# Banked sums, an early schedule and a third batch transposed by DMA in a windowed-attention and feed-forward kernel

## Chip, cores and metric

One core of a Trainium2 chip. The metric is the device time in microseconds (us) of one execution. "Faster" or "slower" needs 2%. Each kernel was profiled once; an instruction is named by its line in that run's kernel, so the same instruction has another line number in another run.

## The reference, cut

```python
# q, k, v: (8 batches, 8 heads, 576 positions, 64); each position sees those within 32
scores = where(|i-j| <= 32, q @ k.T / 8, -1e9);  attn = softmax(scores) @ v
x = attn.transpose(0, 2, 1, 3).reshape(4608, 512)
h = x @ w_in                                     # 512 -> 2048
g = where(h >= 1, h, where(h <= -1, 0, (h + 1) ** 2 / 4))
out = g @ w_out                                  # 2048 -> 512, float32
```

## The kernel before

Attention is woven into the feed-forward part. One pass of the main loop (here: a **slot**, 144 of them and 12 more for the tail) multiplies one 256-wide piece of w_in with 256 tokens (8 matmuls into `hp`), forms g on ScalarE and VectorE, and from slot 12 on adds 4 matmuls of the second product (`op`). Tables say in which slots the pieces of attention come: transposes of q and k, scores, masks, and sums (numerator and denominator of the softmax), whose result goes into `xT`, the left side of the first product.

```python
LONG, NAT = 2, 3            # batches 0, 1: transposed on TensorE from a long layout;
                            # batch 2: on TensorE; batches 3 and up: by DMA
...
def xpose(b, t):            # whole batch, DMA transpose on Sync's queue
    nc.sync.dma_start_transpose(out=qkT(b, t)..., in_=(qn, kn)[t][b]...)
...
def sums(b, y1, lo, hi, pool=ps_n):
    bb = two_banks(pool)    # pool has one buffer: two PSUM banks
    ...                     # matmuls with ones and with v into bb
    def end():
        A.activation(lr, bb[...], AF.Ln); A.activation(rc, lr, AF.Exp, scale=-1.0)
        muls.append(lambda: V.tensor_mul(o, bb[...], rc))   # into xT; done at the next slot's flush()
    return end
...
at(4, None, (0, (0, 1), (0, 2), (2, 4)))                       # slot, sums, scores
at(5, (0, 0, TB, MAIN), (0, (1, 2), (0, 2), (2, 4)))
at(6, (0, 1, TB, MAIN), (0,))
at(7, (0, 0, MAIN, S), None)
sl = [12, 13, 21, 23, 25, 27, 29, 32, 35, 39, ...]             # slots of the later sums
...
for n in range(3):
    tps[22 + n] = [(2, n, t) for t in range(2)]                # batch 2 on TensorE
for b in range(2, B):
    a = 12 if b == 2 else sl[5 * (b - 1) - 1] - 17             # 22 for batch 3, 39 for batch 4
    for t in range(3):
        loads.setdefault(a + t, []).append((b, t))             # q, k, v, issued by GpSimd
    for t in range(2):
        if b >= NAT:
            xps.setdefault(a + 9 + 2 * t, []).append((b, t))   # 31 and 33 for batch 3
...
A.activation(rr, hp, AF.Relu, scale=0.5, bias=0.5)             # every slot
V.tensor_max(hp, hp, rr)                                       # PSUM
V.scalar_tensor_tensor(gT[...], rr, 1.0, hp, op0=ALU.min, op1=ALU.mult)
```

The softmax here doesn't subtract the row's maximum and nothing guards it: scores larger than these inputs give would overflow.

## Time and profile before

| | before |
|---|---|
| median of 4 runs | 331.63 us (329.86 to 333.2) |
| span of the profiled run | 328.8 us |
| TensorE busy | 302.5 us, 92% |
| starts of slots 4, 8, 14, 27, 40 | 26.96, 38.91, 52.42, 84.58, 111.27 us |

The start of a slot is that of its first hp matmul in the trace; all 1152 of them are recorded. Two rows of the table of groups, their columns line, engine, operation, out<-in, shapes and count, then busy us and the mean ns of one, then idle time before them:

```profile
L419 DVE TENSOR_TENSOR hp<-hp,rr 128x512 f32<-128x512 f32 x144 | 100.5, 698 | 45.6 <-ACT rr L418 43.6
L420 DVE SCALAR_TENSOR_TENSOR gT<-rr,hp 128x512 bf16<-128x512 f32 x144 | 98.9, 687 | 4.9
```

They are the two VectorE instructions of each slot, 698 and 687 ns as means, together less than a slot's 1.74 us of matmuls.

### The profile page before, as it was taken

How to read it: one execution, taken by the hardware profiler on the slowest of the kernel's cores; microseconds unless marked ns; L12 is line 12 of the kernel's file. 1: busy time of each engine (PE TensorE's matmuls, PEld its weight loads, DVE VectorE, ACT ScalarE, POOL GpSimd, SP SyncE). 2: the span in 40 equal slices, each digit the busy share in tenths (PEclk: the TensorE clock that was granted, in tenths of full speed). 3: DMA queues.
4: the chain of work that ended last, by engine and by line, in shares of the span. 5: the costliest groups of instructions: out<-in, count | busy, mean ns of one | idle time of the engine just before them, and what ended most of it. 6: DMA issues, size and time to landing. Idle time of an engine off the chain costs nothing.

```text
span 328.8 us, 8409 instructions
## 1 busy us (share of the span) xinstructions
PE 302.5 (92%) x3572; PEld 202.4 (62%) x3615; DVE 227.7 (69%) x346; ACT 195.4 (59%) x320; POOL 140.8 (43%) x138
## 2 busy tenths in 40 slices
PE   7876599997999999999999999998999999999995
PEld 3354466665666666666666666666666666666652
DVE  2345577666678777777777778777677877787830
ACT  3647495675776566755766656665576666644421
POOL 8775717376535482549331962168231322100000
PEclk9989899999999999999999999999999999999999
DMA  7999999969918997699952999339950000010011
GB/s 126 147 171 147 146 205 111 165 64 168 103 52 159 105 131 130 129 106 111 165 84 62 108 157 153 73 50 169 170 106 33 35 34 35 34 63 32 34 64 64
DMA packets 128485, 34.52 MB, mean 105 GB/s; under 512 B 117696, under 2 KB 123584, under 8 KB 128448
## 3 DMA queue, kind: packets, MB, share of 16 engines
q0 software_dynamic: 99584, 18.06, 74.8%
q1 hardware_dynamic: 28864, 15.93, 19.5%
q8 instruction: 28, 0.46, 0.6%
q14 instruction: 9, 0.07, 0.1%
HBM read 36.70 MB, written 9.44 MB: 140 GB/s over the span
## 4 chain that ended last, share of the span: by engine, by line
PE 71%; ACT 8%; POOL 7%; issue 7%; DVE 3%; DMA 3%; ACTq 0%; POOLq 0%
PE hp L414 31%; PE op L432 31%; PE bb L276 5%; DMA w_in<-in_moe_w_in_dram 3%; ACT pt L224 2%; PE bb L216 2%; POOL vn L103 2%; ACT rr L418 1%; PE tp L181 1%; ACT lr L282 1%; DVE hp L419 1%; POOL pt L226 1%; ACT osb L436 1%; DVE gT L420 1%; DVE xT L288 1%
## 5 line engine op out<-in xcount | busy, mean ns | idle before, releaser
L414 PE MATMUL hp<-xT,w_in 128*128 128x256 bf16 x1152 | 151.4, 275 | 8.8 <-DMA w_in<-in_moe_w_in_dram 2.0
L414 PEld LDWEIGHTS <-w_in 128*128 128x128 bf16 x1152 | 111.7, 99 | 52.8 <-issue 9.2
L432 PE MATMUL op<-w_out,gT 128*128 128x512 bf16 x535 | 137.7, 379 | 5.7 <-issue 5.4
L418 ACT ACTIVATE rr<-hp 128x512 f32<-128x512 f32 x144 | 85.6, 595 | 94.2 <-PE hp L414 91.5
L419 DVE TENSOR_TENSOR hp<-hp,rr 128x512 f32<-128x512 f32 x144 | 100.5, 698 | 45.6 <-ACT rr L418 43.6
L420 DVE SCALAR_TENSOR_TENSOR gT<-rr,hp 128x512 bf16<-128x512 f32 x144 | 98.9, 687 | 4.9
L226 POOL TENSOR_TENSOR pt<-pt,mask 128x1024 bf16<-128x1024 bf16 x25 | 53.4, 2138 | 94.3 <-ACT pt L224 89.4
L432 PEld LDWEIGHTS <-gT 128*128 128x128 bf16 x576 | 53.3, 98 | 42.1
L288 DVE TENSOR_TENSOR xT<-bb,rc 128x512 bf16<-128x512 f32 (+1 forms) x32 | 21.0, 657 | 25.0 <-ACT rc L283 25.0
L224 ACT ACTIVATE pt<-bb 128x1024 bf16<-128x1024 f32 (+1 forms) x33 | 33.1, 1010 | 6.2 <-PE bb L216 4.3
L436 ACT COPY osb<-op 128x512 f32<-128x512 f32 x36 | 20.9, 582 | 14.8 <-PE op L432 14.5
L103 POOL DMA_DIRECT2D vn<-in_v_dram x32 | 27.5, 898 | 0.0
L283 ACT ACTIVATE rc<-lr 128x512 f32<-128x512 f32 (+2 forms) x40 | 23.5, 587 | 1.3
L276 PE MATMUL bb<-pt,ones 64*64 64x256 bf16 (+3 forms) x352 | 19.7, 256 | 4.4 <-DVE xT L288 3.6
L282 ACT ACTIVATE lr<-bb 128x512 f32<-128x512 f32 (+2 forms) x40 | 22.0, 550 | 2.1 <-PE bb L276 2.0
L276 PE MATMUL bb<-pt,vn 64*64 64x128 bf16 (+3 forms) x712 | 18.5, 204 | 0.5 <-DMA vn<-in_v_dram 0.5
L276 PEld LDWEIGHTS <-ones 64*64 64x64 bf16 x352 | 10.6, 105 | 13.1 <-issue 10.5
L244 POOL TENSOR_TENSOR pt<-pt,mask 128x384 bf16<-128x384 bf16 x7 | 6.4, 912 | 26.2 <-ACT pt L242 26.2
L276 PEld LDWEIGHTS <-vn 64*64 64x64 bf16 x712 | 16.8, 107 | 0.7 <-DMA vn<-in_v_dram 0.7
L87 POOL DMA_DIRECT2D kn<-in_k_dram x16 | 8.7, 549 | 17.2 <-DMA w_out<-in_moe_w_out_dram 9.1
L95 POOL DMA_DIRECT2D qn<-in_q_dram x12 | 15.0, 1254 | 1.0 <-issue 1.0
L95 POOL DMA_DIRECT2D kn<-in_k_dram x12 | 14.8, 1245 | 0.0
(46 smaller groups left out, 104.5 us busy)
## 6 DMA issues: line engine op xcount, KB each, us to landing
out_dram<-osb SPq DMA_DIRECT2D x36, 256.0 KB, 2.3
vn<-in_v_dram POOLq DMA_DIRECT2D x32, 144.0 KB, 8.1
qn<-in_q_dram POOLq DMA_DIRECT2D x12, 288.0 KB, 6.2
kn<-in_k_dram POOLq DMA_DIRECT2D x12, 288.0 KB, 8.4
w_in<-in_moe_w_in_dram POOLq DMA_DIRECT2D x8, 256.0 KB, 7.7
w_out<-in_moe_w_out_dram POOLq DMA_DIRECT2D x4, 512.0 KB, 11.2
kn<-in_k_dram POOLq DMA_DIRECT2D x16, 72.0 KB, 4.7
qn<-in_q_dram POOLq DMA_DIRECT2D x12, 72.0 KB, 7.7
```

The source lines that it names most:

```text
L95: nc.gpsimd.dma_start(out=x[:, :, h], in_=src[b, NY * h:NY * h + NY].rearrange("y s d -> (y s) d") .rearrange("(u p) d -> p u d", p=128))
L103: nc.gpsimd.dma_start(out=x[64 * a:64 * a + 64, :, h], in_=v[b, y:y + 2].rearrange("y s d -> (y s) d") .rearrange("(c r) d -> r c d", r=64))
L224: A.activation(p, ps[:, :, :128 * n].rearrange(like, y=m), AF.Exp, scale=D ** -0.5)
L226: eng.tensor_mul(p, p, mask4[:, :256 * n].rearrange("p (h j) -> p h j", h=2).rearrange(like, y=m))
L276: nc.tensor.matmul(bb[HD[h], a, o + c0:o + c1], ones[HD[a]] if c is None else vn[b][HD[a], c, h], p(a, h), start=n == 0, stop=True, skip_g ...
L282: A.activation(lr[:, :, :D0], bb[:, :, D0:2 * D0], AF.Ln)
L288: muls.append(lambda: V.tensor_mul(o, bb[:, :, :D0], rc[:, :, :D0]))
L414: nc.tensor.matmul(hp[:, j], w_in[:, kk, 256 * f + 128 * j:256 * f + 128 * j + 128], xT[:, kk, r0:r0 + TB], start=n == 0, stop=n == 3)
L418: A.activation(rr, hp, AF.Relu, scale=0.5, bias=0.5)
L419: V.tensor_max(hp, hp, rr)
L420: V.scalar_tensor_tensor(gT[t][:, 2 * f:2 * f + 2], rr, 1.0, hp, op0=ALU.min, op1=ALU.mult)
L432: nc.tensor.matmul(op, gT[tt // 2][:, ff, 128 * (tt % 2):128 * (tt % 2) + 128], w_out[:, ff], start=ff == 0, stop=ff == 2 * NF - 1)
```

## The change

It is meant to take TensorE's early waits away: sums get a second pair of banks where two follow each other, each transposed part gets its own bank, the early sums move a slot forward, v and the first piece of w_in come sooner, batch 2's transposes leave TensorE, and hp's banks come free one VectorE instruction earlier. The diff, cut:

```diff
-    LONG, NAT = 2, 3
+    LONG = 2
@@ early loads
+    load_v(0, (0,))                      # first half of v ahead of the identity
     make_identity(nc, ident)
-    load_v(0)
-    load_w_in(0)
+    load_v(0, (1,))
+    load_w_in(0, 0, 256)
+    load_w_in(0, 256, 512)
+    load_w_in(1)
     load_long(0, 1, 0)
-    load_w_in(1)
     load_long(0, 1, 1)
@@ schedule
-    at(4, None, (0, (0, 1), (0, 2), (2, 4)))
-    at(5, (0, 0, TB, MAIN), (0, (1, 2), (0, 2), (2, 4)))
-    at(6, (0, 1, TB, MAIN), (0,))
-    at(7, (0, 0, MAIN, S), None)
+    at(4, (scores, 0, (0, 1), (0, 2), (2, 4)), (scores8, 0, ps_n))
+    at(5, (sums, 0, 0, TB, MAIN), (scores, 0, (1, 2), (0, 2), (2, 4)))
+    at(6, (sums, 0, 1, TB, MAIN, ps_s), (sums, 0, 0, MAIN, S))
...
+    at(12, seq[0][0])
+    at(13, (*seq[1][0], ps_s))
+    for n, a in enumerate((20, 22, 25, 29)):       # sums of batch 1's rest, batch 2's first
+        at(a, seq[2 + n][0])
+    for n, a in enumerate((10, 11, 19, 20, 21, 27, 28)):   # scores; batch 2's first at 27, 28
+        at(a, seq[n][1])
...
-    for n in range(3):
-        tps[22 + n] = [(2, n, t) for t in range(2)]
...
-        a = 12 if b == 2 else sl[5 * (b - 1) - 1] - 17
+        a = (12, 26)[b - 2] if b < 4 else sl[5 * (b - 1) - 7] - 17
...
-            if b >= NAT:
-                xps.setdefault(a + 9 + 2 * t, []).append((b, t))
+            xps.setdefault(23 + t if b == 2 else a + 9 + 2 * t, []).append((b, t))
@@ slot
-        eng = None if a < 20 else P
+        eng = None if a < 21 else P
-            V.tensor_max(hp, hp, rr)
-            V.scalar_tensor_tensor(gT[t][:, 2 * f:2 * f + 2], rr, 1.0, hp, op0=ALU.min, op1=ALU.mult)
+            mx = ewp.tile([128, 2, TB], FP, name="mx")
+            V.tensor_max(mx, hp, rr)
+            V.scalar_tensor_tensor(gT[t][:, 2 * f:2 * f + 2], rr, 1.0, mx, op0=ALU.min, op1=ALU.mult)
```

More of the change, by code (lines that the diff above doesn't have):

```diff
@@ L96, in load_nat, with load_v @@
                                 .rearrange("(u p) d -> p u d", p=128))
-    def load_v(b):
-        x = vn[b] = nat.tile([128, 2 * NC, 2, D], BF, name="vn", tag="vn", bufs=3)
-        for h in range(2):
+    def load_v(b, hs=(0, 1)):
+        if b not in vn:
+            vn[b] = nat.tile([128, 2 * NC, 2, D], BF, name="vn", tag="vn", bufs=3)
+        x = vn[b]
+        for h in hs:
             for a in range(2):
@@ L104, in load_v, with load_w_in @@
                                     .rearrange("(c r) d -> r c d", r=64))
-    def load_w_in(n):
-        f = slice(512 * n, 512 * n + 512)
+    def load_w_in(n, c0=0, c1=512):
+        f = slice(512 * n + c0, 512 * n + c1)
         for h in range(2):
@@ L160 @@
     HD = (slice(0, 64), slice(64, 128))
+    HD = (slice(0, 64), slice(64, 128))
     def tpose(b, n, t, copy, ps):
-        o = qkT(b, t)
-        if b < LONG:
-            half, part = divmod(n, 2)
-            j0, j1 = ((0, 5), (5, 9))[part]
-            src = (qn, kn)[t][b, half]
-            dst = o.rearrange("d (y l p j) -> d l y p j", l=2, p=32, j=9)[:, half, :, :, j0:j1]
-            i = ps[:, :j1 - j0].rearrange("d j (y p) -> d y p j", y=NY)
-        else:
-            j0, j1 = 6 * n, 6 * n + 6
-            src = (qn, kn)[t][b].rearrange("p j h d -> p j (h d)")
-            dst = o[:, 128 * j0:128 * j1]
-            i = ps[:, :6].rearrange("d j p -> d (j p)")
+        half, part = divmod(n, 2)
+        j0, j1 = ((0, 5), (5, 9))[part]
+        src = (qn, kn)[t][b, half]
+        dst = qkT(b, t).rearrange("d (y l p j) -> d l y p j", l=2, p=32, j=9)[:, half, :, :, j0:j1]
         for j in range(j0, j1):
-            if len(src.shape) == 3 and b < LONG and src.shape[1] == 2:
+            if src.shape[1] == 2:
                 for h in range(2):
@@ L183, in tpose @@
                 nc.tensor.transpose(ps[:, j - j0], src[:, j], ident)
-        return lambda: copy(dst, i)
+        return lambda: copy(dst, ps[:, :j1 - j0].rearrange("d j (y p) -> d y p j", y=NY))
     def xpose(b, t):
@@ L226, in scores, with scores8 @@
             eng.tensor_mul(p, p, mask4[:, :256 * n].rearrange("p (h j) -> p h j", h=2).rearrange(like, y=m))
-    def scores8(b, eng):
+    def scores8(b, eng, pool=ps_s):
         p = pt8[b] = ptp.tile([128, 2, 2, TAIL], BF, name="pt8")
-        ps = two_banks(ps_s)
+        ps = two_banks(pool)
         if eng is None:
@@ L299, with tp1 @@
     TB = 256
-    def tp1():
-        return ps_h.tile([128, 8, 128], BF, name="tp", tag="hp")
-    def tp2(pool):
-        return pool.tile([128, 2, 8, 128], BF, name="tp", tag="bb")
+    def tp1(pool):
+        if pool is ps_h:
+            return pool.tile([128, 8, 128], BF, name="tp", tag="hp")
+        return pool.tile([128, 2, 8, 128], BF, name="tp", tag="bb")[:, 0]
     def keep_warm(n, pool, tag):
@@ L328 @@
         qn[0, 0] = cast(q32, "qb", 5)
-        qq = [tpose(0, n, 0, (A.copy, V.tensor_copy)[n], tp1()) for n in range(2)]
+        qq = [tpose(0, n, 0, (A.copy, V.tensor_copy)[n], tp1(ps_h)) for n in range(2)]
         for x in qq:
             x()
-        kk = tp2(ps_p)
-        c0, c1 = (tpose(0, n, 1, (A.copy, V.tensor_copy)[n], kk[:, n]) for n in range(2))
+        kk = [tpose(0, n, 1, (A.copy, V.tensor_copy)[n], tp1((ps_n, ps_p)[n])) for n in range(2)]
         keep_warm(3, ps_h, "hp")
-        c0()
-        c1()
+        for x in kk:
+            x()
         for m, n, w in ((mask4, 8, 128), (mask8, 4, TAIL)):
@@ L358, with at @@
     ev, tps = {}, {}
-    def at(a, su, sc):
-        assert a not in ev
-        ev[a] = su, sc
+    def at(a, *todo):
+        ev.setdefault(a, []).extend(x for x in todo if x)
     def steps(b, cut):
@@ L367, in steps @@
             for y1 in range(2):
-                yield (b, y1, lo, hi), (b, (y1, y1 + 1), (0, 2), (2 * k, 2 * k + 2))
-        yield (b, 0, MAIN, S), (b,)
-    at(4, None, (0, (0, 1), (0, 2), (2, 4)))
-    at(5, (0, 0, TB, MAIN), (0, (1, 2), (0, 2), (2, 4)))
-    at(6, (0, 1, TB, MAIN), (0,))
-    at(7, (0, 0, MAIN, S), None)
-    seq = [x for b in range(1, B) for x in steps(b, 224)]
-    sl = [12, 13, 21, 23, 25]
-    sl += [27, 29, 32, 35, 39, 42, 45, 49, 52, 56, 59, 62, 65, 69, 73, 77, 81, 84, 88, 92]
+                yield (sums, b, y1, lo, hi), (scores, b, (y1, y1 + 1), (0, 2), (2 * k, 2 * k + 2))
+        yield (sums, b, 0, MAIN, S), (scores8, b)
+    at(4, (scores, 0, (0, 1), (0, 2), (2, 4)), (scores8, 0, ps_n))
+    at(5, (sums, 0, 0, TB, MAIN), (scores, 0, (1, 2), (0, 2), (2, 4)))
+    at(6, (sums, 0, 1, TB, MAIN, ps_s), (sums, 0, 0, MAIN, S))
+    seq = [x for b in range(1, B) for x in steps(b, 224)]
+    at(12, seq[0][0])
[4 more added lines that the diff above has]
+        at(a, seq[n][1])
+    sl = [30, 32, 35, 39, 42, 45, 49, 52, 56, 59, 62, 65, 69, 73, 77, 81, 84, 88, 92]
     sl += [96, 99, 103, 106, 110, 113, 116, 120, 124, 128]
-    for n, a in enumerate((10, 11, 19, 20)):
-        at(a, None, seq[n][1])
     for n, a in enumerate(sl):
-        nxt = {0: None, 1: None, 2: 4, 3: None}.get(n, n + 1)
-        at(a, seq[n][0], seq[nxt][1] if nxt is not None and nxt < len(seq) else None)
+        at(a, seq[6 + n][0], seq[7 + n][1] if n < len(sl) - 1 else None)
     for a, b, half, t in ((1, 0, 1, 0), (3, 0, 1, 1), (8, 1, 0, 0), (9, 1, 0, 1), (17, 1, 1, 0), (18, 1, 1, 1)):
         tps[a] = [(b, 2 * half + part, t) for part in range(2)]
-    for n in range(3):
-        tps[22 + n] = [(2, n, t) for t in range(2)]
     loads, xps = {}, {}
     for b in range(2, B):
-        a = 12 if b == 2 else sl[5 * (b - 1) - 1] - 17
+        a = (12, 26)[b - 2] if b < 4 else sl[5 * (b - 1) - 7] - 17
         for t in range(3):
@@ L418 @@
             A.activation(rr, hp, AF.Relu, scale=0.5, bias=0.5)
-            V.tensor_max(hp, hp, rr)
-            V.scalar_tensor_tensor(gT[t][:, 2 * f:2 * f + 2], rr, 1.0, hp, op0=ALU.min, op1=ALU.mult)
-        su, sc = ev.get(a, (None, None))
-        end = sums(*su) if su else None
-        if sc:
-            (scores if len(sc) > 1 else scores8)(*sc, eng)
-        if end:
+            mx = ewp.tile([128, 2, TB], FP, name="mx")
+            V.tensor_max(mx, hp, rr)
+            V.scalar_tensor_tensor(gT[t][:, 2 * f:2 * f + 2], rr, 1.0, mx, op0=ALU.min, op1=ALU.mult)
+        ends = []
+        for fn, *x in ev.get(a, []):
+            if fn is sums:
+                ends.append(sums(*x))
+            else:
+                pool = (x.pop(),) if x[-1] in (ps_s, ps_n) else ()
+                fn(*x, eng, *pool)
+        for end in ends:
             end()
@@ L438 @@
         if a in tps:
-            tp = tp2(ps_n if tps[a][0][0] < LONG and tps[a][0][2] else ps_s)
-            copies = [tpose(b, n, t, A.copy if b < LONG else (A.copy, V.tensor_copy)[i], tp[:, i])
+            copies = [tpose(b, n, t, (A.copy, V.tensor_copy)[i if a > LAG else 0], tp1((ps_s, ps_n)[i]))
                       for i, (b, n, t) in enumerate(tps[a])]
```

## The prediction

> **What bounds the kernel now.** I read the page's busy shares first, then the waits, then TensorE's timeline, then the granted clock over short stretches. A slot below is one pass of the main loop (8 matmuls into hp; from slot 12 on also 4 into op); slot n is the n-th pass.
>
> ```profile
> PE 302.5 (92%) x3572; PEld 202.4 (62%) x3615; DVE 227.7 (69%) x346; ACT 195.4 (59%) x320; POOL 140.8 (43%) x138
> ...
> PE 71%; ACT 8%; POOL 7%; issue 7%; DVE 3%; DMA 3%; ACTq 0%; POOLq 0%
> ```
>
> TensorE is busy 92% of the span and is most of the chain that ended last; no other engine is over 69%. So only what TensorE does, or what it waits for, counts. The list of waits says for what (us in total, times, longest):
>
> ```profile
> PE op L432 <- issue: 5.4, 34, 0.2
> PE bb L276 <- DVE xT L288: 3.6, 3, 1.8
> ...
> PE hp L414 <- DMA w_in<-in_moe_w_in_dram: 2.0, 1, 2.0
> PE hp L414 <- DVE xT L288: 1.9, 1, 1.9
> PE hp L414 <- DVE xT L291: 1.8, 1, 1.8
> ...
> PE hp L414 <- issue: 1.6, 1, 1.6
> ```
>
> The first line is no real wait: 34 gaps of 0.16 us where a matmul record is missing (page: 535 op matmuls of 576). The others are real and all early. TensorE's timeline places them:
>
> ```profile
> 33.55 0.29 PE L276 MATMUL bb<-pt,ones 64*64 64x224 bf16 x4 [1.85 <-DVE xT L288]
> ...
> 36.62 0.28 PE L276 MATMUL bb<-pt,ones 64*64 64x192 bf16 x4 [1.31 <-DVE xT L288]
> ...
> 38.91 1.73 PE L414 MATMUL hp<-xT,w_in 128*128 128x256 bf16 x8 [1.80 <-DVE xT L291]
> ...
> 71.73 0.50 PE L183 MATMUL tp<-ident,qn 128*128 128x128 bf16 x6
> 72.06 0.50 PE L183 MATMUL tp<-ident,kn 128*128 128x128 bf16 x6
> 72.40 1.04 PE L414 MATMUL hp<-xT,w_in 128*128 128x256 bf16 x8
> ...
> 77.79 0.81 PE L414 MATMUL hp<-xT,w_in 128*128 128x256 bf16 x6 [1.93 <-DVE xT L288]
> ```
>
> The brackets are idle time of TensorE and what ended it. Twice a sum waits until the multiplication of the sum before has emptied the only pair of banks (33.55, 36.62); twice hp waits for an xT column block that was summed just one slot earlier (38.91, 77.79). After some 90 us there is one real gap over 0.3 us (0.72). The clock adds a loss (columns: stretch, length, busy time of each engine, PEclk, DMA share, GB/s):
>
> ```profile
> 32.00:36.00 4.00, 1.75 (x48) 1.44 (x48) 1.98 (x4) 2.89 (x7) 4.00 (x6) 1.00 1.94 127
> 36.00:39.00 3.00, 0.58 (x29) 0.56 (x29) 2.42 (x4) 1.41 (x3) 2.59 (x5) 1.00 1.33 122
> 39.00:42.00 3.00, 3.00 (x28) 2.04 (x28) 0.70 (x1) 0.82 (x2) 0.54 (x1) 0.51 1.21 192
> ```
>
> TensorE was busy 0.58 of 3 us at 36 to 39, and then ran at 0.51 of its clock.
>
> **What the Trainium skill says.** (1) "TensorE: Matmul & The Clock Gate", Part 1: the clock is halved after an idle window of about 3.4 us and freed after a busy one. The trace agrees: two stretches of 3.41 us at 0.5, from 22.0 and from 39.1 us, each behind a thinly used one. (2) "VectorE: DVE Perf Modes", the perf-mode tier table: fp32 tensor_tensor runs at 1x with SBUF or PSUM operands, 691 ns for 512 elements. The trace has 698 ns for the max, into PSUM; so moving its output to SBUF makes it hardly faster. (3) "DMA: Bandwidth & Descriptors", Issuing engines are not separate DMA queues: DMAs of all issuers share the same engines and interleave. The trace agrees: a 256 KB output takes 2.3 us to landing as the median but up to 7.0 us, where GpSimd's casting loads are in flight. (4) Same page, DMA Transpose: from Sync or Scalar only. The trace has them on Sync's queue:
>
> ```profile
> 96.23 3.29 SPq L188 DMA_TRANSPOSE qT<-qn  x1
> 99.70 2.71 SPq L188 DMA_TRANSPOSE kT<-kn  x1
> ```
>
> **The change part by part.**
>
> *v ahead of the identity; w_in in smaller pieces, w_in(1) before q's half.* The trace of landings shows the DMA engines saturated from 7 us on; slot 4 waits for the third w_in block (landed 26.87, slot starts 26.96; the page calls it "issue"). The bytes ahead of that block stay the same. v's first two issues move from 5.5 to about 3.6 us and fill some 1.2 us of idle DMA time; the smaller w_in pieces have half-size packets and cost perhaps 0.5. The moved block helps slot 2, but the q transposes queued between slots 1 and 2 now wait for q instead. Gain at slot 4: **0.4**.
>
> *Two pairs of banks for sums, and the early sums in fewer slots.* In slot 4 scores8 now uses the sums' banks, slot 6 holds two sums (one per pair), slot 7 none. Following slot 4 at 27.0 with the trace's durations (exp 1.02, Ln 0.54, exp 0.58, xT 0.62, hp 0.87, sum 0.45): slot 5's sum at 30.1, its xT done at 34.0; slot 6's first sum at 32.3 without a wait, its second waits until 34.0 (1.2 remains); slot 7's hp hides part of the last chain; slot 8 starts at 36.7 instead of 38.9. Gain **2.2**, out of 4.96 us of gaps. Slot 13's 0.40 wait goes too: **0.4**.
>
> *Clock.* With slot 8 at 36.7 the window before 39.1 is over half busy, so the half-clock stretch probably goes. It costs 1.6 now (slots 8 and 9 with their transposes: 4.75 us for 3.1 us of work), but scalar copies of the transposes take some back. At 0.7 probability: **0.7**.
>
> *Third batch by DMA.* 36 transposes leave TensorE; each of three groups stands 0.67 us before the next hp (71.73 to 72.40): **2.0**. Also 3 copies of 0.75 us leave ScalarE and 3 of 0.56 VectorE, both off the path.
>
> *Sums of batch 1 one slot earlier* (20 and 22 for 21 and 23): the 1.93 at 77.79 goes, with 0.2 at a kT copy: **2.1**. One more mask is added by TensorE in slot 20: **minus 0.4**.
>
> *max to SBUF:* hp's banks are freed one 0.69 us instruction earlier. TensorE's waits for that (gT) are four of 0.11 to 0.27 us: **0.5**. VectorE's own time is unchanged.
>
> Sum of gains: 0.4+2.2+0.4+0.7+2.0+2.1-0.4+0.5 = **7.9 us**.
>
> *What it costs, first:* scores of batch 2 (slot 27) now need a DMA-made kT. In the built program Sync runs third output, qT, kT in that order, and the output exists only when slot 23 ends. In the trace, output issue (95.71) to kT landing (104.33) took 8.6 us on idle DMA engines, and an output is issued 0.9 us after its last matmul: kT lands 9.5 us after slot 23. TensorE needs it after slots 24 and 26 (1.74 each), 25 (2.3) and hp of 27 (0.87), that is after 6.65 us. **Wait: 2.9**. And engines are not idle: GpSimd has nothing to wait for between its mask in slot 21 and its mask in slot 27, so it runs ahead and issues batch 3's q and k then, though the program lists them at slot 26. They took 12.7 us from first issue (70.97) to last landing before; here about 68 to 80.5, while the transposes start at 72.5. From the late outputs I estimate 3 to 4 us more, 6 to 7 in all, and another half-clock window.
>
> *Second:* batch 3's v issues stand in GpSimd's order between the masks of slots 27 and 28:
>
> ```profile
> 75.84 3.44 POOL L103 DMA_DIRECT2D vn<-in_v_dram  x4
> ```
>
> From kT's landing: scores 0.35, exp 1.0, mask 2.1, v issues 3.4, mask 2.1, some 9.3 us with hand-offs, until slot 30's sum can start. TensorE's work to there is 6.6. **Another 2.6**, or 1.6 if the clock was halved meanwhile, which then hides in it.
>
> Costs: 5.5 uncontended, 8.5 to 10 contended.
>
> **Rivals.** (a) *All gains, no new wait* (transposes land in time): 330.7-7.9 = 323. For it: the author placed the scores three slots behind the transposes. Against: Sync's order and the 8.6 us. (b) *New waits, engines otherwise free:* 330.7-7.9+5.5 = 328.3. (c) *Transposes collide with the loads:* up to 332.8. For it: GpSimd's order and outputs up to 7.0 us. (d) *The start stays DMA-bound, early bank waits return as waits for ScalarE* (its copies for both transposed parts are serial, 1.36 us): adds 1 to 2 to each.
>
> **Range and chances.** I weigh (a) 0.15, (b) 0.35, (c) 0.5: about 329.6. TensorE's steady part, 1.74 us a slot, is the same, and the three runs before spread 2.7 us. Predicted **329.7 us**, range **324.5 to 333.5**. 2% is 6.6 us, so faster means under 324.1: only (a) gives that, **0.10**; slower means over 337.3, beyond (c): **0.03**; within 2%: **0.87**.
>
> **What would show each step.** Right: no wait for xT at slots 5, 8 and 24; slot 8 near 37 us and no 0.5 clock near 40; no transposes at 70 to 80; a new wait of TensorE's batch 2 scores behind kT's DMA near 78 us, and one of a sum for GpSimd's mask near 90, with the v issues before it; the max still near 0.7 us. Wrong: if transposes land within 7 us of slot 23 the result nears 323; if slot 4 starts well before 26 the DMA reading was wrong; if it is over 334, TensorE lost its clock in several windows or the transposes disturb later loads.

## More of the kernel before

Times are medians.

Comparing the starts of equal slots in two traces says at which slot time was won or lost, whatever happened in between.

## The result

The changed kernel takes 348.21 us (347.74 to 348.78, 4 runs) against 331.63: **slower by 5.0%**, ratio 1.0502, 95% interval 1.0439 to 1.0565. (A ratio here is the mean time of one kernel's runs over that of the other's of the same rounds, so not quite the ratio of the medians quoted.) Its profiled span is 347.0 us, 18.2 more than before.

The busy shares and the chain of the page after:

```profile
PE 306.1 (88%) x3540; PEld 203.9 (59%) x3583; DVE 235.9 (68%) x345; ACT 192.1 (55%) x315; POOL 142.0 (41%) x139
...
PE 66%; DMA 10%; POOL 8%; issue 8%; ACT 3%; DVE 2%; SPq 2%; ACTq 0%; POOLq 0%
```

TensorE does fewer matmuls but is busy longer (306.1 us for 302.5): it ran at a lower clock. DMA went from 3% to 10% of the chain. The slot starts say where:

| slot | before | after | difference |
|---|---|---|---|
| 4 | 26.96 | 26.89 | -0.07 |
| 8 | 38.91 | 36.41 | -2.50 |
| 14 | 52.42 | 49.19 | -3.23 |
| 21 | 67.49 | 64.79 | -2.70 |
| 27 | 84.58 | 76.73 | **-7.85** |
| 28 | 87.13 | 88.96 | +1.83 |
| 30 | 91.42 | 94.36 | +2.93 |
| 32 | 94.90 | 102.28 | **+7.38** |
| 39 | 108.79 | 116.10 | +7.31 |
| 42 | 115.02 | 133.50 | **+18.48** |
| 128 | 286.03 | 304.27 | +18.24 |

So 7.85 us were won by slot 27, then 15.2 were lost by slot 32 and 11.2 between slots 39 and 42. TensorE's timeline after (start, length, instruction, and in brackets its idle time and what ended it) has these waits at the places that count:

```profile
33.87 0.28 PE L273 MATMUL bb<-pt,ones 64*64 64x192 bf16 x4 [1.10 <-DVE xT L285]
...
36.41 1.87 PE L407 MATMUL hp<-xT,w_in 128*128 128x256 bf16 x8 [1.07 <-DVE xT L288]
...
86.70 0.64 PE L213 MATMUL bb<-qT,kT 64*64 64x128 bf16 x16 [8.94 <-DMA kT<-kn]
...
97.33 0.29 PE L273 MATMUL bb<-pt,ones 64*64 64x224 bf16 x4 [1.94 <-DVE xT L285]
...
126.11 0.64 PE L213 MATMUL bb<-qT,kT 64*64 64x128 bf16 x16 [8.56 <-DMA kT<-kn]
```

The early waits shrank as intended; slot 30's sum has a new one of 1.94 us, which is taken up with the runs on the max below; the two long new ones are both of scores that wait for a kT made by DMA: batch 2's in slot 27 and batch 3's in slot 39. Sync's queue shows the transposes (here the length is that of the issue):

```profile
72.25 7.72 SPq L185 DMA_TRANSPOSE qT<-qn  x1
80.09 4.59 SPq L185 DMA_TRANSPOSE kT<-kn  x1
...
112.81 5.22 SPq L185 DMA_TRANSPOSE qT<-qn  x1
118.20 5.79 SPq L185 DMA_TRANSPOSE kT<-kn  x1
```

Before, the first pair was issued in 3.29 and 2.71 us. Now each takes 4.6 to 7.7, and the trace has batch 2's qT landing 12.4 us after its issue. What GpSimd did then:

```profile
67.22 0.91 POOL L241 TENSOR_TENSOR pt<-pt,mask 128x384 bf16<-128x384 bf16 x1 [6.44 <-issue]
68.08 2.51 POOL L95 DMA_DIRECT2D qn<-in_q_dram  x2
70.56 2.44 POOL L95 DMA_DIRECT2D kn<-in_k_dram  x2
88.51 2.12 POOL L223 TENSOR_TENSOR pt<-pt,mask 128x1024 bf16<-128x1024 bf16 x1 [15.50 <-ACT pt L221]
90.58 3.45 POOL L105 DMA_DIRECT2D vn<-in_v_dram  x4
94.00 2.18 POOL L223 TENSOR_TENSOR pt<-pt,mask 128x1024 bf16<-128x1024 bf16 x1
...
111.57 2.49 POOL L95 DMA_DIRECT2D qn<-in_q_dram  x2
```

Batch 3's q and k loads are issued at 68 to 73 us, right behind the mask of slot 21, though the program lists them at slots 26 and 27; they are in flight when batch 2's transposes start at 72.25. Batch 4's q loads start at 111.57, a microsecond ahead of batch 3's transposes at 112.81. And v's issues stand between the masks of slots 27 and 28. Last, the granted clock (stretch, length, busy time by engine, PEclk, DMA share, GB/s):

```profile
77.00:80.50 3.50, 0.77 (x8) 0.44 (x5) 2.46 (x4) 0.60 (x1) 0.00 (x0) 1.00 1.85 142
80.50:84.00 3.50, 0.00 (x0) 0.00 (x0) 0.00 (x0) 0.00 (x0) 0.00 (x0) 0.50 1.44 158
84.00:87.50 3.50, 0.80 (x17) 0.53 (x18) 0.00 (x0) 0.10 (x1) 0.00 (x0) 0.50 0.72 140
87.50:91.00 3.50, 3.50 (x25) 1.72 (x26) 0.00 (x0) 1.60 (x3) 2.49 (x2) 0.53 0.10 39
```

While TensorE waits, nothing else computes, only DMA runs. Its clock is halved at 80.5 and stays so for 10.24 us, four of them after the wait was over.

### The profile page after: what moved, and what is told of

It reads as the page before. It is cut to its first block, busy times and chain, and to the rows that moved or that the text cites. A ratio compares the mean times of both kernels' runs of the same rounds, so it can differ in the third digit from the quotient of the medians.

```text
span 347.0 us, 8347 instructions
## 1 busy us (share of the span) xinstructions
PE 306.1 (88%) x3540; PEld 203.9 (59%) x3583; DVE 235.9 (68%) x345; ACT 192.1 (55%) x315; POOL 142.0 (41%) x139
## 4 chain that ended last, share of the span: by engine, by line
PE 66%; DMA 10%; POOL 8%; issue 8%; ACT 3%; DVE 2%; SPq 2%; ACTq 0%; POOLq 0%
PE op L429 30%; PE hp L407 29%; PE bb L273 4%; DMA kT<-kn 4%; DMA w_in<-in_moe_w_in_dram 4%; POOL vn L105 3%; PE bb L213 2%; SPq L185 2%; DMA qn<-in_q_dram 2%; POOL w_in L111 1%; DVE mx L413 1%; POOL pt L223 1%; ACT pt L221 1%; DVE gT L414 1%; POOL kn L87 1%
## 5 line engine op out<-in xcount | busy, mean ns | idle before, releaser
L407 PE MATMUL hp<-xT,w_in 128*128 128x256 bf16 x1152 | 153.6, 278 | 2.6 <-DVE xT L288 1.1
L429 PE MATMUL op<-w_out,gT 128*128 128x512 bf16 x535 | 140.7, 386 | 6.1 <-issue 5.7
L407 PEld LDWEIGHTS <-w_in 128*128 128x128 bf16 x1152 | 113.9, 100 | 47.6 <-issue 5.7
L413 DVE TENSOR_TENSOR mx<-hp,rr 128x512 f32<-128x512 f32 x144 | 99.1, 688 | 52.4 <-ACT rr L411 51.1
L414 DVE SCALAR_TENSOR_TENSOR gT<-rr,mx 128x512 bf16<-128x512 f32 x144 | 110.8, 769 | 4.9
L213 PE MATMUL bb<-qT,kT 64*64 64x128 bf16 x520 | 13.8, 226 | 17.5 <-DMA kT<-kn 17.5
L213 PEld LDWEIGHTS <-kT 64*64 64x64 bf16 x520 | 9.7, 112 | 19.4 <-DMA kT<-kn 17.9
L87 POOL DMA_DIRECT2D kn<-in_k_dram x16 | 8.7, 548 | 18.5 <-DMA w_in<-in_moe_w_in_dram 6.9
```

The source lines that it names most:

```text
L213: nc.tensor.matmul(ps[HD[a], h, 128 * n:128 * n + 128], kT[b][HD[h], s0:s0 + 64], qTs[b % 3][HD[h], PAD + s0 - 32:PAD + s0 + 96], start=en ...
L407: nc.tensor.matmul(hp[:, j], w_in[:, kk, 256 * f + 128 * j:256 * f + 128 * j + 128], xT[:, kk, r0:r0 + TB], start=n == 0, stop=n == 3)
L413: V.tensor_max(mx, hp, rr)
L414: V.scalar_tensor_tensor(gT[t][:, 2 * f:2 * f + 2], rr, 1.0, mx, op0=ALU.min, op1=ALU.mult)
L429: nc.tensor.matmul(op, gT[tt // 2][:, ff, 128 * (tt % 2):128 * (tt % 2) + 128], w_out[:, ff], start=ff == 0, stop=ff == 2 * NF - 1)
```

## Experiments

The theory (**C**): two waits for a DMA-made kT make the loss, because the transposes share the DMA engines with GpSimd's loads; with them come half-clock and the masks behind v's issues. Rivals: **B**, the new bank rotation and slots themselves cost time; **S**, transposes behind Sync's outputs are late whatever the loads do. The kernel before ran beside all of them: median 331.68 us (7 runs) beside b3_early, before_b3_late, both_early and b2_pe, and 332.17 (11 runs, on another chip) beside the other four. So kernels of the two groups are compared by their ratios to before. The results of all are correct.

### b3_early: batch 3's transposes where they were

```diff
-            xps.setdefault(23 + t if b == 2 else a + 9 + 2 * t, []).append((b, t))
+            xps.setdefault((23 + t, 31 + 2 * t)[b - 2] if b < 4 else a + 9 + 2 * t, []).append((b, t))
```

> The changed kernel with one edit: batch 3's two DMA transposes back at slots 31 and 33 (as before the change), from 35 and 37. Theory C (the loss is two waits for a kT whose transposes share the DMA engines with GpSimd's loads): they then run before batch 4's loads, kT of batch 3 lands before slot 39, the 8.6 us wait and the half-clock that follows go, about 11 us: 337 us (335.5 to 338.5). The wait of batch 2 (8.9) stays. Rival B (the loss lies in the new bank rotation and slots): no change, 348.

Measured: 337.39 us (336.51 to 338.96), ratio to before 1.0175 (1.0135 to 1.0215). The transposes are issued in 3.58 and 2.68 us, the wait of slot 39 is gone, batch 2's wait stays (9.79 here). Undoing the shift of batch 3 by four slots takes off 10.8 us, as C has it.

### before_b3_late: the same edit alone, on the kernel before

```diff
-                xps.setdefault(a + 9 + 2 * t, []).append((b, t))
+                xps.setdefault((35 if b == 3 else a + 9) + 2 * t, []).append((b, t))
```

> The kernel before with one edit: batch 3's transposes moved from slots 31 and 33 to 35 and 37, nothing else of the change. Theory C: Sync issues them behind the output of slot 35 (105 us), a microsecond after batch 4's q loads start (104.3), kT lands near 117 and is needed at 109.7: a wait of 7 to 9 us and 1 to 2 of half-clock, 340 us (338 to 342). Rival B: 331.6, since four slots are still left for two transposes of 5 us.

Measured: 341.73 us (341.08 to 343.47), ratio 1.0318 (1.0275 to 1.0361). TensorE's timeline and Sync's queue of this run:

```profile
117.95 0.64 PE L216 MATMUL bb<-qT,kT 64*64 64x128 bf16 x16 [8.49 <-DMA kT<-kn]
```

```profile
104.71 5.56 SPq L188 DMA_TRANSPOSE qT<-qn  x1
110.45 5.39 SPq L188 DMA_TRANSPOSE kT<-kn  x1
```

The same long issues and the same wait, 8.49 us, in a kernel that has nothing else of the change. One number in a table makes 10 us. B is not needed for this part. Not all of it is sharing: an undisturbed pair of transposes took 7.6 us from first issue to last landing in b3_loads_late (below) and 8.4 in b3_early. By an estimate from these, a pair issued at 104.71 lands at 112.3 to 113.1, and TensorE, idle from 109.46, waits some 3 us all the same. That batch 4's loads make the rest is read from the long issues and from the test of batch 2 that follows; those loads were not moved themselves.

### b3_loads_late: no loads beside batch 2's transposes

```diff
-            loads.setdefault(a + t, []).append((b, t))
+            loads.setdefault(a + t + (3 if b == 3 else 0), []).append((b, t))
```

> The changed kernel with batch 3's loads three slots later (29, 30, 31 in place of 26, 27, 28), so GpSimd can't issue them before the masks of slots 27 and 28, and batch 2's transposes at 23 and 24 have the DMA engines to themselves. Theory C: transposes are issued in 3 us each instead of 7.7 and 4.6, kT lands 9.5 us after slot 23 and TensorE waits 2.9 (2 to 4) in place of 8.9, without 10 us of half-clock. Rival S (transposes this slow by themselves): 8 to 9. The collision of batch 3's transposes with batch 4's q stays; the mask of slot 30 now stands behind q and k, some 3 us. In all 342 us (339 to 345).

Measured: 340.38 us (339.52 to 341.58), ratio 1.0266 (1.0222 to 1.031). Sync's queue and TensorE's timeline:

```profile
72.16 2.91 SPq L185 DMA_TRANSPOSE qT<-qn  x1
75.19 2.74 SPq L185 DMA_TRANSPOSE kT<-kn  x1
```

```profile
79.79 0.47 PE L213 MATMUL bb<-qT,kT 64*64 64x128 bf16 x16 [2.12 <-DMA kT<-kn]
```

Issued at the same time as in the changed kernel (72.16 for 72.25), behind the same output, the two transposes now land at 79.74 us instead of 86.66, and the wait is 2.12 us instead of 8.94. Some 7 us of that wait come from sharing and 2 from Sync's order: S is true, but small. Batch 3's collision stays (9.90 us), and the loads held back delay a later mask (1.51 us wait), so the total is no gain worth having.

### both_early: all transposes earlier

Batch 2's transposes go to slots 19 and 20, batch 3's to 31 and 33.

```diff
-            xps.setdefault(23 + t if b == 2 else a + 9 + 2 * t, []).append((b, t))
+            xps.setdefault((19 + t, 31 + 2 * t)[b - 2] if b < 4 else a + 9 + 2 * t, []).append((b, t))
```

> The changed kernel with batch 2's transposes at slots 19 and 20 (from 23, 24) and batch 3's at 31 and 33. Theory C: batch 2's kT still shares the engines with v of batch 2 and q of batch 3 but has seven slots, and lands near 75 us, before it is needed at 77.6: both waits go. Left: the wait of slot 30's sum for GpSimd's mask behind the v issues, 2 to 3 us. 331.6-7.9-0.5+2.5 = 326 us (324 to 328). Rival S (transposes behind outputs on Sync are late whatever the loads do): batch 2's kT comes 3 us late or more, 329 to 333.

Measured: 334.5 us (334.06 to 335.62), ratio 1.0088 (1.0054 to 1.0121). **A miss**: 326 was expected.

```profile
62.64 7.08 SPq L185 DMA_TRANSPOSE qT<-qn  x1
69.82 8.44 SPq L185 DMA_TRANSPOSE kT<-kn  x1
```

```profile
84.16 0.64 PE L213 MATMUL bb<-qT,kT 64*64 64x128 bf16 x16 [6.98 <-DMA kT<-kn]
```

Asked for 9.6 us earlier than in the changed kernel, kT lands only 2.5 earlier (84.12 for 86.66). From 62 us on it shares the engines with batch 2's v and then with batch 3's q and k, which suffer in turn: k's last piece lands at 88.1 instead of 84.5. Starting a transpose sooner does not help while loads keep coming; my own expectation had counted free slots and not bytes in flight. (The expectation named 329 to 333 for S, but the test above shows the loads to be the cause.)

### b2_pe: everything but the third batch by DMA

Batch 2 goes back to TensorE (slots 22 to 24, both parts in one pair of banks) and batch 3's transposes to 31 and 33; the rest of the change stays.

```diff
+    for n in range(3):
+        tps[22 + n] = [(2, n, t) for t in range(2)]
...
-            xps.setdefault(23 + t if b == 2 else a + 9 + 2 * t, []).append((b, t))
+            if b > 2:
+                xps.setdefault(31 + 2 * t if b == 3 else a + 9 + 2 * t, []).append((b, t))
```

> The changed kernel with batch 2 transposed on TensorE again (slots 22 to 24, one pair of banks) and batch 3's transposes at 31 and 33: every part of the change but the third batch by DMA. Theory C: 331.6-7.9+2.0 (36 transposes) -0.5, plus the mask behind the v issues (1.5 to 2.5): 327 us (325.5 to 329). Rival B (banks, slots, w_in or max cost time themselves): over 331.

Measured: 329.35 us (328.69 to 330.31), ratio 0.993 (0.9896 to 0.9963). The sign is as C has it; the size is 2.4 us short, just outside the range expected (325.5 to 329). Slot 27 starts 5.8 us earlier than before the change, so B falls; but from slot 30 to 31 it loses 5.2 us. TensorE and GpSimd there:

```profile
89.50 0.40 PE L281 MATMUL bb<-pt,ones 64*64 64x224 bf16 x4 [2.95 <-POOL pt L231]
```

```profile
81.47 2.44 POOL L231 TENSOR_TENSOR pt<-pt,mask 128x1024 bf16<-128x1024 bf16 x1 [8.40 <-ACT pt L229]
83.86 3.45 POOL L105 DMA_DIRECT2D vn<-in_v_dram  x4
87.27 2.17 POOL L231 TENSOR_TENSOR pt<-pt,mask 128x1024 bf16<-128x1024 bf16 x1
```

GpSimd idles 8.4 us, does one mask, then spends 3.45 us on issuing loads, and only then does the mask that slot 30's sum waits for. A half-clock stretch (from 89.0 us, 3.41 long) comes with the end of the wait.

### b2_pe_v: v's load ahead of the masks

```diff
-            loads.setdefault(a + t, []).append((b, t))
+            loads.setdefault(a if b == 3 else a + t, []).append((b, t))
```

> The kernel of run b2_pe with one edit: batch 3's v load at slot 26 with its q and k, so that GpSimd issues it ahead of the masks of slots 27 and 28. Theory P (the 2.95 us wait of slot 30's sum and the half-clock stretch after it come from the v issues between two masks): slot 31 loses its 5.2 us, 324.3 us (323 to 325.5), 2.2% under the kernel before. Rival (the sum waits for the slower mask, 2.1 us, itself): 328 or more.

Measured: 326.79 us (325.63 to 328.82), ratio 0.9857 (0.9815 to 0.9899). GpSimd now uses its idle time for the issues:

```profile
72.93 3.44 POOL L105 DMA_DIRECT2D vn<-in_v_dram  x4
81.37 4.97 POOL L231 TENSOR_TENSOR pt<-pt,mask 128x1024 bf16<-128x1024 bf16 x2 [5.00 <-ACT pt L229]
```

Slot 31 starts 3.4 us earlier than in b2_pe, without the half-clock stretch. P holds in its place, but the time misses the range expected (323 to 325.5): by the ratios, b2_pe_v is 0.7% (some 2.4 us) under b2_pe, and the two intervals just meet. A wait of 1.03 us for xT is left at the same sum; the next runs show where it comes from.

### b2_pe_v_psum and before_mx: the max to SBUF by itself

b2_pe_v with the max back in PSUM, and the kernel before with the max in SBUF alone:

```diff
-            mx = ewp.tile([128, 2, TB], FP, name="mx")
-            V.tensor_max(mx, hp, rr)
-            V.scalar_tensor_tensor(gT[...], rr, 1.0, mx, op0=ALU.min, op1=ALU.mult)
+            V.tensor_max(hp, hp, rr)
+            V.scalar_tensor_tensor(gT[...], rr, 1.0, hp, op0=ALU.min, op1=ALU.mult)
```

> b2_pe_v with the max written to PSUM as before the change. If the SBUF max frees hp's banks usefully: 0.5 to 1 us slower than b2_pe_v. If its longer second instruction (769 ns for 687) costs what it frees: same within 0.3 us.

> The kernel before with the max to SBUF alone. The prediction had minus 0.5 us (four waits for gT gone). VectorE gains 80 ns per slot, 11.5 us of busy time in all, off the path: 331.2 us (330.6 to 332); if VectorE's extra time reaches the path, over 332.5.

Measured: b2_pe_v_psum 326.06 us (324.72 to 326.59), ratio to before 0.9825 (0.979 to 0.986), 0.7 us under b2_pe_v, which neither branch of its expectation had; the intervals overlap. before_mx 332.16 us (330.52 to 332.56), ratio 1.0005 (0.9969 to 1.0041). The max to SBUF gains nothing in either kernel. The groups of the changed kernel, then minimum, median and maximum (ns) of the second instruction, then VectorE's timeline around slot 30's sum:

```profile
L413 DVE TENSOR_TENSOR mx<-hp,rr 128x512 f32<-128x512 f32 x144 | 99.1, 688 | 52.4 <-ACT rr L411 51.1
L414 DVE SCALAR_TENSOR_TENSOR gT<-rr,mx 128x512 bf16<-128x512 f32 x144 | 110.8, 769 | 4.9
...
L414 DVE SCALAR_TENSOR_TENSOR gT<-rr,mx x144: 691/692/2234, 19.3 to 333.3; 128x512 bf16<-128x512 f32 x144
...
94.51 2.23 DVE L414 SCALAR_TENSOR_TENSOR gT<-rr,mx 128x512 bf16<-128x512 f32 x1
96.67 0.61 DVE L285 TENSOR_TENSOR xT<-bb,rc 128x448 bf16<-128x448 f32 x1
```

The max takes 10 ns less. The second instruction, now with two SBUF inputs, has a mean of 769 ns, but the mean hides two kinds: 132 of the 144 take 691 to 716 ns (686 to 690 before), and twelve take 1.10 to 2.23 us. Each of the twelve runs beside one of GpSimd's masks and ends 0.54 to 0.56 us after it, as here (mask from 94.00 to 96.18 us, instruction to 96.74). Of the seven kernels with the max in SBUF, 98 of these instructions take over 750 ns, 97 of them beside a mask like this. In the three with it in PSUM (before, before_b3_late, b2_pe_v_psum) none of 432 takes over 690 ns, though 114 run beside a mask. So it is not a longer instruction, as the expectation had it, but one that is held until the mask is over.

What VectorE has to do next is then late: slot 30's sum waits for xT for 1.03 us in b2_pe_v and for 0.40 in b2_pe_v_psum. In before_mx TensorE's waits of hp for VectorE did not go either: 1.1 us in two (for the max) in place of 0.6 in three (for gT).

b2_pe_v_psum is the fastest version found, 1.75% under the kernel before (interval 1.4 to 2.1%), so not shown to pass the 2%.

## Why the prediction was wrong

**The gains were right in sum, in part by luck.** By slot 27 the prediction had 7.4 us (its 7.9 without the max, which is spread over the whole run); the trace has 7.85. Step by step: the start, 0.4 predicted, gave 0.07, less than the scatter (slot 4 starts at 26.17 to 26.99 in the three traces with the start of before); the early sums, 2.2, gave 2.4; slot 13, 0.4, gave 0.46; the mask on TensorE cost 0.2 instead of 0.4 (slots 20 and 21 together, since a sum moved from one to the other); and the third batch with the earlier sums, 4.1, gave 4.7, of it 2.0 for the 36 transposes (slots 22 to 27 take 11.89 us in b2_pe, 9.88 here), and 0.6 only because batch 2's first scores moved from slot 25 to 27.

The clock, 0.7, gave 0.3 by slot 11, since this trace has a half-clock stretch all the same, at 36.2 instead of 39.1. But that is the exception: the other six traces with the changed start have none between 31 and 79 us, and their slots 8 to 11 take 5.05 to 5.07 us, against 6.35 here and 6.62 in all three traces with the start of before. The stretch did go as a rule, and was worth the 1.6 us that the prediction gave for it. A half-clock stretch in one trace can be that execution's alone.

The max, 0.5, gave nothing (before_mx). "VectorE's own time is unchanged" was wrong: beside a GpSimd mask the instruction after the max was held, for up to 2.23 us in place of 0.69.

**The step that failed is the costs, "5.5 uncontended, 8.5 to 10 contended", in two ways.**

1. *A whole term is missing.* The costs ask only what happens to batch 2. Batch 3's transposes also moved, from slots 31 and 33 to 35 and 37, and there batch 4's q loads start. This was in the diff (22 became 26) and in the landings of before (batch 4's q at 104 us, kT of batch 3 landing at 104.3, just ahead of it); I did not ask it of every batch. Its wait came to 8.56 us, and slots 39 to 42 lose 11.2 us in the trace; b3_early takes 10.8 off the time by undoing it, and before_b3_late puts 10 on by doing it alone.
2. *Batch 2's terms were too small.* From slot 27 to 32 the trace loses 15.2 us against at most 10. Mechanism and place of the first wait were as told: Sync's order, and GpSimd running ahead with batch 3's loads. "6 to 7 in all" measured 8.94. The term that was too small is the delay by the loads, "3 to 4 us more", taken from late outputs: it measured 6.9 (kT landing at 86.66 for 79.74 in b3_loads_late). qT's issue alone grew from 3.3 to 7.7 us and pushed kT's. "Another half-clock window" was 10.24 us, which still halved TensorE's clock for 4 us after the wait, and a second one of 3.41 us came with slot 30's wait. That wait, "another 2.6", measured 1.94, and its end was not as told: the mask behind v's issues ended at 96.18, 0.8 us into the wait, but xT, held up behind the VectorE instruction that this mask had held, was done only at 97.3.

The uncontended estimate held: the prediction's 2.9 us measured 2.12 with the loads away (b3_loads_late). Rival (c), the collision, was the right one; it had a weight of 0.5, and at most 10 us of costs where 26.4 were lost. The prediction's own sign of being wrong, "if it is over 334", named what the trace then showed: half-clock stretches at 80.5, 97.6 and 121.5 us, and transposes that disturb later loads (batch 4's q landed 9.4 and 11.5 us after issue, 6.3 before).

**Why the change lost although TensorE was given less to do.** 36 transposes were worth some 2 us of TensorE. Even in b3_loads_late, where no load runs beside them, slot 28 starts 0.9 us later than in b2_pe, where TensorE does them: the wait for kT and the clock cost more than the work. *Open:* how the DMA engines divide themselves between the two queues, and so why loads and transposes delay each other by just this much; the runs show the delay, not its inside. Nor do they separate the bank rotation, the earlier sums and the w_in pieces by a timed run each; only slot starts do. And no run has batch 2 on DMA with both collisions removed.

## What to carry to other kernels

When work moves from the bounding engine to DMA, list every transfer in flight at that time, for every later iteration that the new table shifts, and check it against the landing times of the trace before. GpSimd's queue ran ahead of the place where the program lists its instructions: batch 3's q load, listed in slot 26 (75.0 us), was issued at 68.1, as soon as the mask before it was done; and v's load, listed between two masks, delayed the second by 3.45 us. A wait of several microseconds on TensorE costs more than itself: after the one of 8.94 us the clock stayed halved for 4 us. And before a mean duration explains anything, look at the median and the maximum: here 769 ns was 692 with twelve exceptions.

## What the Trainium skill lacked or had wrong

- "DMA: Bandwidth & Descriptors", Issuing engines are not separate DMA queues: it says that DMAs of all engines interleave, which the runs agree with, but gives no cost for it. Here a DMA transpose pair took 7.6 us from first issue to last landing alone (72.16 to 79.74), 14.4 beside batch 3's q and k loads (72.25 to 86.66), and 21.5 beside batch 2's v and batch 3's q and k (62.64 to 84.12).
- Same section: the time to initiate a DMA "is usually small relative to the DMA itself". That holds for one v load in b2_pe (issued in 0.9 us, landed 3.8 to 4.8 us after), but it leaves out that GpSimd computes nothing meanwhile: four in a row kept a mask waiting 3.45 us and TensorE 2.95 us.
- "VectorE: DVE Perf Modes", the perf-mode tier table has no row for scalar_tensor_tensor. Here fp32 of 512 elements took 687 ns with one input in PSUM and 692 ns with both in SBUF (median), or up to 2.6 us where a GpSimd mask ran beside it (before_mx).
